# K tiles transposed as pairs of fp32 words, and a direct PV product, in a one-token decode kernel

## The chip, the core and the metric

The kernel runs on one core of one Trainium2 chip. The metric is the device time of one execution in microseconds; a time below is of one execution or the median of several. All inputs are bfloat16 and lie in HBM.

## What is computed

One token of a transformer block for a batch of B = 2: attention over a cache, then a gated feed-forward. The cache is what is large: K and V are each 2 x 32 heads x 8192 positions x 128 values, 134 MB each.

```
h  = x + A(layernorm(x))
q  = x @ wq                        -> [B, 32 heads, 1, 128]
s  = q . k_cache * 128**-0.5       -> [B, 32, 1, 8192]
o  = softmax(s) @ v_cache          -> [B, 32, 1, 128]
A  = o.reshape(B, 1, 4096) @ wo    (wo: 4096 x 512)
h2 = h + W_down(relu(W_gate(layernorm(h))) * W_up(layernorm(h)))     (F = 1376)
```

## The kernel before

**Tiling.** The work is cut into NP = 32 pairs; pair p is two neighbouring heads of one batch. The K tile of a pair has 128 partitions, 64 for each head; a partition holds J = 128 consecutive positions of its head, each with 128 values, so a tile is 128 x 32 KB = 4 MB, loaded by one DMA with 32 KB a partition. V has the same form. Four slots of SBUF hold tiles: K of even and odd pairs, V of even and odd pairs.

**Scores on two engines.** Of the J = 128 positions of a partition, 96 go to VectorE in NCH = 2 halves of JC = 48: a product with the broadcast q (L407), a tree of additions (L415), a reduction (L424). The other JP = 32 go to TensorE in NG = 4 groups of GT = 8 (L427 to L444): 8 transposes of 128x128 into a PSUM tile `Tp` (L434), one ScalarE copy to `kT` in SBUF (L440), and in `score_group` (L274) 8 products with `kT` as the stationary operand and two columns of q (`qT`) as the moving one. Two `Tp` tiles alternate, and three `kT`.

**Softmax and PV.** `exp` (L282) runs on ScalarE, part by part (the 32 positions of TensorE, then VectorE's halves), and writes `e_t`, two columns a position, one for each head, with zeros on the other head's partitions. `pv` (L341) multiplies it with V: for four positions at a time, the 8 columns of `e_t` are the stationary operand and 512 columns of V the moving one (L361); 32 such products of a pair go to four 32-row strips of a PSUM bank `Op`. Of each 8 x 512 result only the blocks are wanted in which position meets position. `collect` (L368), called one pair later, copies `Op` to SBUF in fp32 (`os_sb`, L372), and four fp32 products with a selecting matrix `sel` (L378) add the blocks into two columns of the bank `Ob`. For the last pair, `pv` takes the other form already: V's 128 x 128 blocks stationary, two columns of `e_t` moving (L354).

**Normalization and the rest.** After pairs 8, 16, 24 and 31, `z_sum` (L293) adds the exponentials' sums over the partitions with a product by ones, `normalize` (L300) reduces and inverts them on VectorE, and `o_scale` (L314) writes the scaled outputs `O_sb`. `o_proj` (L324) multiplies them with wo: for the first 24 heads after pair 24, for the rest at the end. Then come the residual, the feed-forward's products (L518, L560) and the output.

**The order of work.** The engines' instruction streams are written out by hand. Each engine runs its instructions in program order; `Prog` gives each engine a semaphore that counts its instructions, and `wait` makes an engine wait for another's count. All loads but x are issued by SyncE (SP) on one DMA queue, in this order:

- wq, K0, V0, K1, V1, a piece of W_down; then wo (L226) when the q product is done with wq's place;
- in the loop, for pair p: K of p+2 (L459 to L461), when the second VectorE product of p (L407) and the last transpose of p are done (`t_kfree`); then V of p+2 (`load_v`, L387), when `pv(p)` is done (`t_pv`);
- at pair 30: the weights W_up and W_gate in slot 0, V of pair 31 in four parts with semaphores of their own (`vparts`, L338), W_down.

**The last pairs.** In pair 31, `pv(30)` and `collect(30)` are issued after the TensorE scores and the first `exp` of pair 31 (L450 to L453), and `normalize(3)` stands within VectorE's tree of additions for the last half (L418). After the loop: `o_proj` for heads 24 to 31 without the last pair's batch, `z_sum` and `normalize` of the last pair, `pv(31)`, and what follows from it.

The two statements that differ most:

```
i = nc.tensor.transpose(Tp[n % 2][:, k * 128:(k + 1) * 128], k_t[:, j, :], ident[:])             # L434, x8 a group
i = nc.tensor.matmul(o[g:g + 2 * VJ, :], lhsT=e_t[p % 2][:, j:j + VJ, :]..., rhs=v_t[:, j:j + VJ, :]...)   # L361, x32 a pair
```

Of the kernel before, what the change touches and what calls it, by code (L numbers as in the profile page):

```python
# [6 lines left out]
F32 = mybir.dt.float32  # L7
BF16 = mybir.dt.bfloat16
ALU = mybir.AluOpType
ACT = mybir.ActivationFunctionType  # L10
# [28 lines left out]
def bass_sequential_preLN__gqa_block_cached__glu_gated_reglu__decode_kernel(  # L39
# [12 lines left out]
    B, _, D = A_x.shape  # L52
# [14 lines left out]
    VJ = 4  # L67
# [4 lines left out]
    with ExitStack() as es:  # L72
# [27 lines left out]
        qT = sb("qT", [128, NP * 2], BF16)  # L100
        ident = sb("ident", [128, 128], BF16)
# [47 lines left out]
        with nc.Block() as block:  # L149

            @block.sync
            def _(eng):
# [18 lines left out]
                pool.run(nc.gpsimd.memset(sel[:], 0.0))  # L171
                for c in range(4):
                    pool.last()
                    pool.run(nc.gpsimd.tensor_copy(
                        out=sel[32 * c:32 * c + 2 * VJ, :], in_=ident_f[0:2 * VJ, 0:2 * VJ]))
                pool.last()
# [24 lines left out]
                for k, row in enumerate((x_row, lnx_row)):  # L201
                    rv = row.rearrange("b (n c) -> b c n", c=DC)
                    for c in range(DC):
                        i = nc.tensor.transpose(
                            Tp[0][:, (k * DC + c) * B:(k * DC + c + 1) * B], rv[:, c, :], ident[0:B, 0:B])
                t = pe.run(i)
                dve.wait(t)
                t_xlT = dve.run(nc.vector.tensor_copy(out=xlT[:], in_=Tp[0][:, 0:2 * DC * B]))
# [6 lines left out]
                for h in range(H):  # L215
# [8 lines left out]
                    in_=Wp[:, 0:H * B].rearrange("p (g a b) -> p g b a", b=B, a=2)))  # L224
                sp.wait(t_q)
# [34 lines left out]
                t_os, t_ob = {}, {}  # L260
# [6 lines left out]
                def score_group(p, g):  # L267
                    n = p * NG + g
                    pe.wait(t_ev[n])
# [17 lines left out]
                def zbank(k):  # L287
                    return Sp[0] if k == 4 else Ob

                def zcol(k):  # L290
                    return 64 if k == 4 else 2 * NP

                def z_sum(k, p0, p1):  # L293
                    pe.wait(t_exp[p1 - 1][-1])
                    t = pe.run(nc.tensor.matmul(  # L295
                        zbank(k)[:, zcol(k):zcol(k) + (p1 - p0) * 2 * (NCH + 1)], lhsT=ones_f[:],
                        rhs=zs[:, 2 * p0:2 * p1, :], start=True, stop=True))
                    return t

                def normalize(k, p0, p1, t, split):  # L300
                    n = 2 * (p1 - p0)
                    dve.wait(t)
                    dve.run(nc.vector.tensor_reduce(
                        out=zr[:, 2 * p0:2 * p1],
                        in_=zbank(k)[:, zcol(k):zcol(k) + n * (NCH + 1)].rearrange("p (n k) -> p n k", k=NCH + 1),
                        axis=AX.X, op=ALU.add))
                    dve.last()
                    dve.run(nc.vector.reciprocal(out=zi[:, 2 * p0:2 * p1], in_=zr[:, 2 * p0:2 * p1]))
                    dve.last()
                    if split:  # L310
                        return None
                    return o_scale(k, p0, p1)

                def o_scale(k, p0, p1):  # L314
                    src = Op[1][:, 0:2] if k == 4 else Ob[:, 2 * p0:2 * p1]
                    return dve.run(nc.vector.tensor_tensor(
                        out=O_sb[:, 2 * p0:2 * p1], in0=src, in1=zi[:, 2 * p0:2 * p1],
                        op=ALU.mult))
# [22 lines left out]
                def pv(p):  # L341
                    v_t = tile((2 * p + 1) % 4)
                    o = Op[p % 2]
                    parts = vparts if p == NP - 1 else (
                        [(0, NCH * JC, J)] + [(1 + c, c * JC, (c + 1) * JC) for c in range(NCH)])
                    pe.wait(t_zero)
                    if p >= 2:
                        pe.wait(t_os[p - 2])
                    nmm = 0
                    for ci, (ei, j0, j1) in enumerate(parts):  # L350
                        pe.wait(t_exp[p][ei], (sem_vl[ci], 16) if p == NP - 1 else t_v[p])
                        if p == NP - 1:
                            for j in range(j0, j1):
                                i = nc.tensor.matmul(  # L354
                                    o[:, 0:2], lhsT=v_t[:, j, :], rhs=e_t[p % 2][:, j, :],
                                    start=(nmm == 0), stop=(nmm == J - 1))
                                nmm += 1
                            continue
                        for j in range(j0, j1, VJ):
                            g = 32 * (nmm % 4)  # L360
                            i = nc.tensor.matmul(  # L361
                                o[g:g + 2 * VJ, :], lhsT=e_t[p % 2][:, j:j + VJ, :].rearrange("p j a -> p (j a)"),
                                rhs=v_t[:, j:j + VJ, :].rearrange("p j d -> p (j d)"),
                                start=(nmm < 4), stop=(nmm >= J // VJ - 4))
                            nmm += 1
                    t_pv[p] = pe.run(i)

                def collect(p):  # L368
                    act.wait(t_pv[p])
                    if p >= 1:  # L370
                        act.wait(t_ob[p - 1])
                    t_os[p] = act.run(nc.scalar.activation(out=os_sb[:], in_=Op[p % 2][:], func=ACT.Copy))  # L372
                    k = next(kk for kk, (a, b_) in enumerate(batches) if a <= p < b_)
                    pe.wait(t_os[p])
                    if p == batches[k][0] and k >= 1:
                        pe.wait(t_O[k - 1])
                    for jj in range(VJ):
                        i = nc.tensor.matmul(  # L378
                            Ob[:, 2 * p:2 * p + 2], lhsT=os_sb[:, jj * Dh:(jj + 1) * Dh],
                            rhs=sel[:, 2 * jj:2 * jj + 2], start=(jj == 0), stop=(jj == VJ - 1))  # L380
                    t_ob[p] = pe.run(i)
# [17 lines left out]
                for p in range(NP):  # L399
# [3 lines left out]
                    for c in range(NCH):  # L403
                        dve.wait(t_k[p])
                        dve.last()
# [4 lines left out]
                        while w > 8:  # L410
# [7 lines left out]
                            if p == NP - 1 and c == 1 and w == Dh // 2:  # L418
                                t_O[3] = normalize(3, 24, 31, t_batch[3], False)
# [5 lines left out]
                        if c == 0:  # L425

                            pe.wait(t_k[p])  # L427
                            for g in range(NG):
                                n = p * NG + g
                                if n >= 2:  # L430
                                    pe.wait(t_ev[n - 2])
                                for k in range(GT):
                                    j = NCH * JC + g * GT + k
                                    i = nc.tensor.transpose(  # L434
                                        Tp[n % 2][:, k * 128:(k + 1) * 128], k_t[:, j, :], ident[:])
                                t_pt[n] = pe.run(i)
# [3 lines left out]
                                t_ev[n] = act.run(nc.scalar.activation(  # L440
                                    out=kT[n % 3][:], in_=Tp[n % 2][:], func=ACT.Copy))
# [8 lines left out]
                            if p == NP - 1:  # L450
                                pv(p - 1)
                            if p >= 1:
                                collect(p - 1)  # L453
# [29 lines left out]

                pe.wait(t_O[3])
# [121 lines left out]
```

## Time and profile before

| | us |
|---|---|
| three runs | 672.58, 672.62, 673.44 |
| median | 672.62 |
| the profiled execution: its time | 672.58 |
| its span in the profile | 670.7 |
| busy in the span: VectorE (DVE) | 494.4 (74%) |
| TensorE products (PE), its weight loads (PEld) | 352.0 (52%), 234.1 (35%) |
| ScalarE (ACT) | 220.1 (33%) |
| GpSimd (POOL) | 2.5 |
| data loaded | 281.06 MB |

The span runs from the program's first instruction to its last; 1.9 us of the time lie outside it. Busy time is the sum of an engine's instructions. TensorE's products and its weight loads are counted apart and overlap each other. The costliest groups, with the mean duration of one instruction:

| line | engine | what | count | busy us | mean ns |
|---|---|---|---|---|---|
| L407 | DVE | product with q, 128x6144 | 64 | 214.9 | 3358 |
| L440 | ACT | copy of transposed K, 128x1024 | 128 | 126.2 | 1021 |
| L434 | PE | transposes, 128x128 bf16 | 1024 | 122.0 | 305 |
| L361 | PE | PV, 8 columns stationary, 512 moving | 992 | 116.3 | 621 |
| L378 | PE | fp32 products of `collect` (two records for each call) | 248 | 57.5 | 354 |
| L274 | PE | scores, two moving columns | 1024 | 48.2 | 168 |
| L372 | ACT | copy of `Op`, 128x512 fp32 | 31 | 18.5 | 597 |
| L354 | PE | PV of the last pair, two moving columns | 128 | 3.7 | 166 |

Means of TensorE are from an instruction's start to its modelled end. Products follow each other faster than that: 8 transposes take 1.01 us in the timeline, 80 products of L354 take 2.27 us.

### The profile page before, as it was taken

The page shows a single profiled execution, that of the slowest core. Times are in us where ns is not written, and L with a number is a line of the kernel's source. Part 1 is how long each engine was busy: PE and PEld are TensorE (multiplying, and loading weights), DVE is VectorE, ACT ScalarE, POOL GpSimd, SP SyncE. Part 2 cuts the span into 40 slices and gives each one's busy share as a digit, 9 for nine tenths or more (in the row PEclk, how much of TensorE's full clock was granted, in tenths as well). Part 3 has the DMA queues.
Part 4 walks back from the last instruction along what each step waited for, and adds up shares of the span by engine and source line. Part 5 has one row for each costly group of instructions (what it writes and reads, how often), then busy time and mean ns, then how long its engine had stood idle before and what let it go on. Part 6 is the DMA issues. An engine that isn't in the chain of part 4 may idle for free.

```text
span 670.7 us, 8986 instructions
## 1 busy us (share of the span) xinstructions
PE 352.0 (52%) x3868; PEld 234.1 (35%) x3868; DVE 494.4 (74%) x430; ACT 220.1 (33%) x554; POOL 2.5 (0%) x16
## 2 busy tenths in 40 slices
PE   2553355455545455554554655454556565455655
PEld 2431333233433223343322433232234443223435
DVE  1774477788768678877777887677786977678792
ACT  0631322233432234344222333322333342233340
POOL 1000000000000000000000000000000000000000
PEclk9999999665565555655556656655566555565555
DMA  9999999999999999999999999999999999999994
GB/s 375 434 436 357 434 435 430 427 431 429 434 433 427 428 433 433 425 436 425 434 433 427 431 436 424 431 432 431 437 426 425 434 432 433 426 430 431 428 409 146
DMA packets 15915, 281.63 MB, mean 420 GB/s; under 512 B 1442, under 2 KB 6916, under 8 KB 7044
## 3 DMA queue, kind: packets, MB, share of 16 engines
q1 hardware_dynamic: 15872, 281.06, 98.4%
q8 instruction: 30, 0.49, 0.3%
q14 instruction: 9, 0.07, 0.0%
q10 hardware_dynamic: 4, 0.00, 0.0%
HBM read 281.05 MB, written 0.00 MB: 419 GB/s over the span
## 4 chain that ended last, share of the span: by engine, by line
DMA 72%; DVE 22%; PE 3%; ACT 2%; issue 1%; SPq 0%; DVEq 0%
DMA slot<-in_A_k_cache_dram 68%; DVE prod L407 14%; DVE tb L415 4%; DMA slot<-in_A_v_cache_dram 3%; DVE prod L415 2%; ACT kT L440 1%; DVE scores L424 1%; PE T L434 1%; PE Ob L378 1%; ACT e L282 0%; PE S L274 0%; ACT os_sb L372 0%; PE Ob L295 0%; PE S L518 0%; PE O L560 0%
## 5 line engine op out<-in xcount | busy, mean ns | idle before, releaser
L407 DVE TENSOR_TENSOR prod<-slot,q_b 128x6144 bf16<-128x6144 bf16 x64 | 214.9, 3358 | 128.2 <-DMA slot<-in_A_k_cache_dram 126.9
L361 PE MATMUL O<-slot,e 128*8 128x512 bf16 x992 | 116.3, 621 | 143.4 <-ACT e L282 127.8
L440 ACT ACTIVATE kT<-T 128x1024 bf16<-128x1024 bf16 x128 | 126.2, 1021 | 160.2 <-PE T L434 159.4
L434 PE MATMUL T<-ident,slot 128*128 128x128 bf16 x1024 | 122.0, 305 | 65.3 <-DMA slot<-in_A_k_cache_dram 65.3
L415 DVE TENSOR_TENSOR tb<-prod 128x3072 bf16<-128x3072 bf16 (+1 forms) x128 | 148.2, 1158 | 4.4
L434 PEld LDWEIGHTS T<-ident,slot 128*128 128x128 bf16 x1024 | 99.3, 140 | 92.3 <-DMA slot<-in_A_k_cache_dram 90.6
L282 ACT ACTIVATE e<-scores 64x48 bf16<-64x48 f32 x128 | 32.8, 256 | 239.2 <-DVE scores L424 237.6
L361 PEld LDWEIGHTS O<-slot,e 128*8 128x8 bf16 x992 | 24.0, 106 | 209.6 <-ACT e L282 155.6
L415 DVE TENSOR_TENSOR prod<-tb 128x1536 bf16<-128x1536 bf16 (+1 forms) x128 | 84.2, 658 | 4.4
L378 PE MATMUL Ob<-sel,os_sb 128*128 128x2 f32 x248 | 57.5, 354 | 47.7 <-ACT os_sb L372 47.7
L378 PEld LDWEIGHTS Ob<-sel,os_sb 128*128 128x128 f32 x248 | 54.9, 327 | 51.2 <-ACT os_sb L372 51.2
L274 PE MATMUL S<-qT,kT 128*128 128x2 bf16 x1024 | 48.2, 168 | 39.2 <-ACT kT L440 38.1
L274 PEld LDWEIGHTS S<-qT,kT 128*128 128x128 bf16 x1024 | 40.7, 106 | 57.5 <-ACT kT L440 57.5
L424 DVE TENSOR_REDUCE scores<-prod 128x48 f32<-128x384 bf16 x64 | 35.4, 553 | 2.2
L282 ACT ACTIVATION_READ_ACCUMULATOR e<-scores 64x1 f32 x128 | 23.6, 185 | 0.0
L372 ACT ACTIVATE os_sb<-O 128x512 f32<-128x512 f32 x31 | 18.5, 597 | 3.4 <-PE O L361 2.7
L282 ACT ACTIVATE e<-S 64x32 bf16<-64x32 f32 x64 | 12.9, 202 | 15.0 <-PE S L274 14.2
L282 ACT ACTIVATION_READ_ACCUMULATOR e<-S 64x1 f32 x64 | 12.8, 201 | 0.7
L251 ACT ACTIVATE q_b<-O 128x512 bf16<-128x512 f32 x8 | 4.3, 595 | 15.8 <-PE O L246 15.8
L222 DVE CAST qT<-W 128x64 bf16<-128x64 f32 x1 | 0.2, 224 | 12.2 <-PE W L217 12.2
L217 PE MATMUL W<-xlT,X 128*128 128x2 bf16 x128 | 3.6, 166 | 8.8 <-DMA X<-in_A_wq_dram 8.8
L217 PEld LDWEIGHTS W<-xlT,X 128*128 128x128 bf16 x128 | 3.5, 104 | 8.8 <-DMA X<-in_A_wq_dram 8.8
(67 smaller groups left out, 58.8 us busy)
## 6 DMA issues: line engine op xcount, KB each, us to landing
slot<-in_A_k_cache_dram SPq DMA_DIRECT2D x32, 4096.0 KB, 27.7
slot<-in_A_v_cache_dram SPq DMA_DIRECT2D x31, 4096.0 KB, 31.3
X<-in_A_wq_dram SPq DMA_DIRECT2D x1, 4096.0 KB, 12.5
X<-in_A_wo_dram SPq DMA_DIRECT2D x1, 4096.0 KB, 48.7
slot<-in_A_v_cache_dram SPq DMA_DIRECT2D x1, 1536.0 KB, 19.8
slot<-in_B_W_up_dram SPq DMA_DIRECT2D x1, 1376.0 KB, 10.0
slot<-in_B_W_gate_dram SPq DMA_DIRECT2D x1, 1376.0 KB, 14.6
slot<-in_A_v_cache_dram SPq DMA_DIRECT2D x1, 1280.0 KB, 22.2
```

The source lines that it names most:

```text
L217: i = nc.tensor.matmul(Wp[:, h * B:(h + 1) * B], lhsT=wq[:, c, h * Dh:(h + 1) * Dh], rhs=lT[:, c * B:(c + 1) * B], start=(c == 0), stop=(c ...
L251: t_cp[m] = act.run(nc.scalar.activation(out=q_b[:, m * 512:(m + 1) * 512], in_=Op[m % 2][:], func=ACT.Copy))
L274: i = nc.tensor.matmul(Sp[p % 2][:, 2 * jj:2 * jj + 2], lhsT=kT[n % 3][:, k * 128:(k + 1) * 128], rhs=qT[:, 2 * p:2 * p + 2], start=True, ...
L282: t = act.run(nc.scalar.activation(out=e_t[p % 2][q, j0:j0 + nj, a], in_=src(q, a), func=ACT.Exp, scale=inv_sqrt_dh, accum_out=zs[q, 2 * p ...
L361: i = nc.tensor.matmul(o[g:g + 2 * VJ, :], lhsT=e_t[p % 2][:, j:j + VJ, :].rearrange("p j a -> p (j a)"), rhs=v_t[:, j:j + VJ, :].rearrang ...
L372: t_os[p] = act.run(nc.scalar.activation(out=os_sb[:], in_=Op[p % 2][:], func=ACT.Copy))
L378: i = nc.tensor.matmul(Ob[:, 2 * p:2 * p + 2], lhsT=os_sb[:, jj * Dh:(jj + 1) * Dh], rhs=sel[:, 2 * jj:2 * jj + 2], start=(jj == 0), stop= ...
L407: t_dm = dve.run(nc.vector.tensor_tensor(out=prod[:], in0=k_t[:, c * JC:(c + 1) * JC, :], in1=qv, op=ALU.mult))
L415: dve.run(nc.vector.tensor_tensor(out=o, in0=cur[:, :, 0:half], in1=cur[:, :, half:w], op=ALU.add))
L424: t_s = dve.run(nc.vector.tensor_reduce(out=sc[:], in_=cur, axis=AX.X, op=ALU.add))
L434: i = nc.tensor.transpose(Tp[n % 2][:, k * 128:(k + 1) * 128], k_t[:, j, :], ident[:])
L440: t_ev[n] = act.run(nc.scalar.activation(out=kT[n % 3][:], in_=Tp[n % 2][:], func=ACT.Copy))
```

## The change

**Transposes.** Two positions of a K tile, 2 x 128 bf16 values, are taken as 128 fp32 words and transposed by one fp32 transpose with the fp32 identity, 4 a group in place of 8. In the result, row n holds the values 2n and 2n+1 of the even position's head vector in rows 0 to 63 and of the odd position's in rows 64 to 127. `Tp` becomes three fp32 tiles (`Ob`'s bank is free now), read by the same copy as bf16.

**Scores.** For each two positions there are two products, r = 0 for even and r = 1 for odd places in the head vector, accumulated into four columns (two positions x two heads). The moving operand is `q2`, 4 columns for each pair and r: q's even or odd values in rows 0 to 63 for the first position and in rows 64 to 127 for the second, and zeros elsewhere. `q2` is made at the start by four products with every second column of the identity, a memset and four copies on VectorE. The number of products is as before, 8 a group.

**PV.** All pairs take the form that only the last one had: V's 128 x 128 block of each position stationary, two columns of `e_t` moving, 128 products of a pair, accumulated into the pair's two columns of `Op[k % 2]` for its batch k. `collect`, `os_sb`, `sel`, `Ob` and the memsets of `Op` are gone. `z_sum` and `normalize` of a batch now follow `pv` of its last pair directly; in the last pair, `pv(30)` and `normalize(3)` come after the loop.

The diff, cut to its core:

```diff
+        q2 = sb("q2", [128, NP, 2, 4], BF16)
-        os_sb = sb("os_sb", [128, 512], F32)
-        sel = sb("sel", [128, VJ * 2], F32)
-        Tp = [ps(f"T{i}", [128, GT * 128], BF16) for i in range(2)]
+        Tp = [ps(f"T{i}", [128, GT * 64], F32) for i in range(3)]
-        Ob = ps("Ob", [128, 512], F32)
...
+                pe.wait(t_qT)
+                for r in range(2):
+                    for h in range(2):
+                        i = nc.tensor.matmul(
+                            Sp[r][64 * h:64 * h + 64, 0:2 * NP], lhsT=ident[:].rearrange("p (n r) -> p r n", r=2)[:, r, :],
+                            rhs=qT[:], start=True, stop=True)
+                t = pe.run(i)
+                dve.run(nc.vector.memset(q2[:], 0.0))
+                dve.wait(t)
+                dve.last()
+                for r in range(2):
+                    for h in range(2):
+                        t_q2 = dve.run(nc.vector.tensor_copy(
+                            out=q2[64 * h:64 * h + 64, :, r, 2 * h:2 * h + 2],
+                            in_=Sp[r][64 * h:64 * h + 64, 0:2 * NP].rearrange("p (n a) -> p n a", a=2)))
...
-                dve.wait(t_cp[NP // 4 - 2], t_cp[NP // 4 - 1])
-                for o in Op:
-                    t_zero = dve.run(nc.vector.memset(o[:], 0.0))
...
-                    for k in range(GT):
-                        jj = g * GT + k
-                        i = nc.tensor.matmul(
-                            Sp[p % 2][:, 2 * jj:2 * jj + 2], lhsT=kT[n % 3][:, k * 128:(k + 1) * 128],
-                            rhs=qT[:, 2 * p:2 * p + 2], start=True, stop=True)
+                    kv_ = kT[n % 3][:].rearrange("p (k n r) -> p k r n", n=128, r=2)
+                    for k in range(GT // 2):
+                        jj = g * GT + 2 * k
+                        for r in range(2):
+                            i = nc.tensor.matmul(
+                                Sp[p % 2][:, 2 * jj:2 * jj + 4], lhsT=kv_[:, k, r, :],
+                                rhs=q2[:, p, r, :], start=(r == 0), stop=(r == 1))
...
-                        for j in range(j0, j1, VJ):
-                            g = 32 * (nmm % 4)
+                        for j in range(j0, j1):
                             i = nc.tensor.matmul(
-                                o[g:g + 2 * VJ, :], lhsT=e_t[p % 2][:, j:j + VJ, :].rearrange("p j a -> p (j a)"),
-                                rhs=v_t[:, j:j + VJ, :].rearrange("p j d -> p (j d)"),
-                                start=(nmm < 4), stop=(nmm >= J // VJ - 4))
+                                Op[k % 2][:, col:col + 2], lhsT=v_t[:, j, :], rhs=e_t[p % 2][:, j, :],
+                                start=(nmm == 0), stop=(nmm == J - 1))
                             nmm += 1
                     t_pv[p] = pe.run(i)
-
-                def collect(p):
-                    act.wait(t_pv[p])
...
-                    t_os[p] = act.run(nc.scalar.activation(out=os_sb[:], in_=Op[p % 2][:], func=ACT.Copy))
...
-                    if p + 1 in ends:
+                    if p + 1 in ends and p < NP - 1:
                         t_batch[k] = z_sum(k, *batches[k])
...
+                        if p == 0 and c == 0:
+                            dve.wait(t_cp[NP // 4 - 1])
...
-                            if p == NP - 1 and c == 1 and w == Dh // 2:
-                                t_O[3] = normalize(3, 24, 31, t_batch[3], False)
...
-                                if n >= 2:
-                                    pe.wait(t_ev[n - 2])
-                                for k in range(GT):
-                                    j = NCH * JC + g * GT + k
+                                if n >= 3:
+                                    pe.wait(t_ev[n - 3])
+                                for k in range(GT // 2):
+                                    j = NCH * JC + g * GT + 2 * k
                                     i = nc.tensor.transpose(
-                                        Tp[n % 2][:, k * 128:(k + 1) * 128], k_t[:, j, :], ident[:])
+                                        Tp[n % 3][:, k * 128:(k + 1) * 128],
+                                        k_t[:, j:j + 2, :].rearrange("p j d -> p (j d)").bitcast(F32), ident_f[:])
...
-                            if p == NP - 1:
-                                pv(p - 1)
-                            if p >= 1:
-                                collect(p - 1)
...
+                pv(NP - 2)
+                t_O[3] = normalize(3, 24, 31, t_batch[3], False)
                 pe.wait(t_O[3])
```

More of the change, by code (lines that the diff above doesn't have):

```diff
@@ L66, in bass_sequential_preLN__gqa_block_cached__glu_gated_reglu__decode_kernel @@
     FR = F - 10 * 128
-    VJ = 4
     eps = 1e-5
@@ L170, in _ @@
                 pool.run(nc.gpsimd.memset(onesn[:], 1.0 / D))
[L171 to L176, printed above, removed]
                 for e in e_t:
@@ L204, in _ @@
                         i = nc.tensor.transpose(
-                            Tp[0][:, (k * DC + c) * B:(k * DC + c + 1) * B], rv[:, c, :], ident[0:B, 0:B])
+                            Tp[0][:].bitcast(BF16)[:, (k * DC + c) * B:(k * DC + c + 1) * B], rv[:, c, :], ident[0:B, 0:B])
                 t = pe.run(i)
                 dve.wait(t)
-                t_xlT = dve.run(nc.vector.tensor_copy(out=xlT[:], in_=Tp[0][:, 0:2 * DC * B]))
+                t_xlT = dve.run(nc.vector.tensor_copy(out=xlT[:], in_=Tp[0][:].bitcast(BF16)[:, 0:2 * DC * B]))
                 xT = xlT[:, 0:DC * B]
@@ L252, in _ @@
                         out=q_b[:, m * 512:(m + 1) * 512], in_=Op[m % 2][:], func=ACT.Copy))
-                dve.wait(t_cp[NP // 4 - 2], t_cp[NP // 4 - 1])
-                for o in Op:
-                    t_zero = dve.run(nc.vector.memset(o[:], 0.0))
                 t_pt, t_ev, t_sc, t_pv = {}, {}, {}, {}
-                t_os, t_ob = {}, {}
                 t_exp = {}
@@ L268, in score_group @@
                     n = p * NG + g
-                    pe.wait(t_ev[n])
+                    pe.wait(t_ev[n], t_q2)
                     if g == 0 and p >= 2:
                         pe.wait(t_exp[p - 2][0])
-                    for k in range(GT):
-                        jj = g * GT + k
-                        i = nc.tensor.matmul(
-                            Sp[p % 2][:, 2 * jj:2 * jj + 2], lhsT=kT[n % 3][:, k * 128:(k + 1) * 128],
-                            rhs=qT[:, 2 * p:2 * p + 2], start=True, stop=True)
+                    kv_ = kT[n % 3][:].rearrange("p (k n r) -> p k r n", n=128, r=2)
[5 more added lines that the diff above has]
+                                rhs=q2[:, p, r, :], start=(r == 0), stop=(r == 1))
                     t_sc[n] = pe.run(i)
@@ L287, in zbank @@
                 def zbank(k):
-                    return Sp[0] if k == 4 else Ob
-                def zcol(k):
-                    return 64 if k == 4 else 2 * NP
+                    return Sp[0] if k == 4 else Op[k % 2]
                 def z_sum(k, p0, p1):
@@ L295, in z_sum @@
                     t = pe.run(nc.tensor.matmul(
-                        zbank(k)[:, zcol(k):zcol(k) + (p1 - p0) * 2 * (NCH + 1)], lhsT=ones_f[:],
+                        zbank(k)[:, 64:64 + (p1 - p0) * 2 * (NCH + 1)], lhsT=ones_f[:],
                         rhs=zs[:, 2 * p0:2 * p1, :], start=True, stop=True))
@@ L304, in normalize @@
                         out=zr[:, 2 * p0:2 * p1],
-                        in_=zbank(k)[:, zcol(k):zcol(k) + n * (NCH + 1)].rearrange("p (n k) -> p n k", k=NCH + 1),
+                        in_=zbank(k)[:, 64:64 + n * (NCH + 1)].rearrange("p (n k) -> p n k", k=NCH + 1),
                         axis=AX.X, op=ALU.add))
@@ L314, in o_scale @@
                 def o_scale(k, p0, p1):
-                    src = Op[1][:, 0:2] if k == 4 else Ob[:, 2 * p0:2 * p1]
                     return dve.run(nc.vector.tensor_tensor(
-                        out=O_sb[:, 2 * p0:2 * p1], in0=src, in1=zi[:, 2 * p0:2 * p1],
+                        out=O_sb[:, 2 * p0:2 * p1], in0=Op[k % 2][:, 0:2 * (p1 - p0)], in1=zi[:, 2 * p0:2 * p1],
                         op=ALU.mult))
@@ L342, in pv @@
                     v_t = tile((2 * p + 1) % 4)
-                    o = Op[p % 2]
+                    k = next(kk for kk, (a, b_) in enumerate(batches) if a <= p < b_)
+                    col = 2 * (p - batches[k][0])
                     parts = vparts if p == NP - 1 else (
                         [(0, NCH * JC, J)] + [(1 + c, c * JC, (c + 1) * JC) for c in range(NCH)])
-                    pe.wait(t_zero)
-                    if p >= 2:
-                        pe.wait(t_os[p - 2])
+                    if p == batches[k][0] and k >= 2:
+                        pe.wait(t_O[k - 2])
                     nmm = 0
@@ L351, in pv @@
                         pe.wait(t_exp[p][ei], (sem_vl[ci], 16) if p == NP - 1 else t_v[p])
-                        if p == NP - 1:
[L353 to L358, printed above, removed]
-                        for j in range(j0, j1, VJ):
-                            g = 32 * (nmm % 4)
+                        for j in range(j0, j1):
                             i = nc.tensor.matmul(
-                                o[g:g + 2 * VJ, :], lhsT=e_t[p % 2][:, j:j + VJ, :].rearrange("p j a -> p (j a)"),
-                                rhs=v_t[:, j:j + VJ, :].rearrange("p j d -> p (j d)"),
-                                start=(nmm < 4), stop=(nmm >= J // VJ - 4))
+                                Op[k % 2][:, col:col + 2], lhsT=v_t[:, j, :], rhs=e_t[p % 2][:, j, :],
+                                start=(nmm == 0), stop=(nmm == J - 1))
                             nmm += 1
                     t_pv[p] = pe.run(i)
-                def collect(p):
-                    act.wait(t_pv[p])
-                    if p >= 1:
-                        act.wait(t_ob[p - 1])
-                    t_os[p] = act.run(nc.scalar.activation(out=os_sb[:], in_=Op[p % 2][:], func=ACT.Copy))
[L373 to L381, printed above, removed]
-                    if p + 1 in ends:
+                    if p + 1 in ends and p < NP - 1:
                         t_batch[k] = z_sum(k, *batches[k])
@@ L440, in _ @@
                                 t_ev[n] = act.run(nc.scalar.activation(
-                                    out=kT[n % 3][:], in_=Tp[n % 2][:], func=ACT.Copy))
+                                    out=kT[n % 3][:], in_=Tp[n % 3][:].bitcast(BF16), func=ACT.Copy))
                                 if g >= 1:
@@ L449, in _ @@
                                 NCH * JC, JP)
-                            if p == NP - 1:
-                                pv(p - 1)
-                            if p >= 1:
-                                collect(p - 1)
                         act.wait(t_s)
```

## The prediction

> **What bounds the kernel now.** I read first the slices and the queues of the page, to see which resource has no idle time.
>
> ```profile
> DMA  9999999999999999999999999999999999999994
> ...
> q1 hardware_dynamic: 15872, 281.06, 98.4%
> q8 instruction: 30, 0.49, 0.3%
> ```
>
> The transfers fill every slice but the last: 281.06 MB, 98.4% of all 16 DMA engines' time. The second queue row matters below: 30 packets of 16 KB of instructions, 0.3% of 16 x 670.7 us = 32 us, so 1.07 us each.
>
> Second, stretches of three pairs each, inside the loop (columns: length; busy time and count of PE, PEld, DVE, ACT, POOL; TensorE clock; DMA share; GB/s).
>
> ```profile
> 218.32:276.61 58.29, 31.24 (x313) 20.03 (x312) 44.25 (x36) 20.05 (x51) 0.00 (x0) 0.53 1.00 431
> 276.61:334.90 58.29, 31.73 (x312) 20.41 (x312) 44.78 (x36) 19.56 (x51) 0.00 (x0) 0.51 1.00 430
> ```
>
> DMA share 1.00; DVE is busy 44.8 of 58.3 us, PE 31.7, ACT 20. One pair (8.39 MB) takes 19.43 us, and DVE idles about 4.5 us in it, PE about 9. No compute engine sets the pace.
>
> Third, the chain that ended last, where DVE starts on K tiles 10, 12, 14, 18, 20, 22, 24, 26, 28, 30 right after they land (columns: start, length, what):
>
> ```profile
> 232.31 3.37 DVE prod L407
> ...
> 271.16 3.37 DVE prod L407
> ...
> 310.02 3.37 DVE prod L407
> ...
> 388.25 3.37 DVE prod L407
> ...
> 428.14 3.37 DVE prod L407
> ...
> 467.00 3.37 DVE prod L407
> ...
> 506.33 0.05 issue
> ...
> 545.24 3.37 DVE prod L407
> ...
> 585.12 3.37 DVE prod L407
> ...
> 623.98 3.37 DVE prod L407
> ```
>
> The clean step for two pairs is 38.86 us (232.31 to 271.16, 271.16 to 310.02). But 310.02 to 388.25 is 0.51 us more than two such steps, 388.25 to 428.14 is 1.03 more, 467.00 to 506.33 is 0.47 more, 545.24 to 585.12 is 1.02 more: 391.67 us for ten steps where 388.6 would do. Some 3.1 us are lost, in jumps. The trace's DMA packets tell why. For a whole load, the moments at which the 16 DMA engines finished their shares (us after the first of them), by when the last finished:
>
> ```
>  42.97  0.00 0.09 0.10 0.14 0.16 0.18 0.28 0.36 0.40 0.40 0.42 0.45 0.66 0.82 1.64 1.78
> 211.37  0.00 0.11 0.33 0.37 0.38 0.41 0.85 1.18 1.70 1.71 1.73 1.85 1.85 2.02 2.16 2.37
> 222.11  0.00 0.12 0.32 0.37 0.38 0.41 0.86 1.18 1.70 1.72 1.72 1.85 2.01 2.17 2.38 3.40
> 623.50  0.00 0.07 0.12 0.16 0.28 0.59 2.80 4.02 4.58 4.68 4.82 4.85 5.16 5.39 6.24 6.41
> ```
>
> Between rows two and three lies one instruction packet, at 215.7 us, and one engine went from 1.85 to 3.40. Each such packet costs its engine 1.54 us (the 1.08 us packet, and 0.48 us by which a 32 KB data packet beside it is longer than its usual 1.22). An engine never makes this up, as all 16 stream without a gap, and a load has landed only when the slowest is done. From 43.0 to 623.5 us the slowest engine fell back 4.63 us, during 24 packets of PE instructions: **0.193 us a packet**. That is 1.54/8: followed from load to load, the jumps go round some eight engines, while six stay within 0.6 us. So the kernel's time is its data at 9.714 us per 4 MB load, plus what instruction packets take from the unluckiest engine, plus a start and a tail.
>
> **The change, part by part.** I add to the profiled execution: span 670.7, timed at 672.58 us (the lowest; the median of the three is 672.62).
>
> *TensorE's instructions.* The page counts 3868 matmuls and as many weight loads; 7736 / 30 = 258 a packet, so a packet holds 256. Removed: 992 wide PV products (L361), 248 records of the 124 fp32 products of `collect` (L378), 512 of the 1024 transposes. Score products stay 1024 (L274: before 8 a group, after 4 x 2). Added: 31 x 128 = 3968 PV products and 4 for q2. New count 3868 - 992 - 248 - 512 + 3968 + 4 = 6088, with weight loads 12176, so 4440 instructions more: **17.3 packets**. The trace shows no fp32 transpose. If it has two records a call, as L378 has, the count is 21.3 packets; if one, as L434, 17.3. I take one: L434 is the same operation. Price: 17.3 x 0.193 = **+3.3 us**. Spread over all 16 engines it would be 17.3 x 1.54 / 16 = +1.7; with 21.3 packets and a third hit on the slowest engine, 3 x 1.54 = +4.6.
>
> The Trainium skill speaks against this term. "Runtime: NRT & Kernel Launch", section "Instruction fetch mechanics", has the refill in blocks of 256 instructions, as the packets here, and calls the cost of crossing a block "mostly hidden". That is said of the engine that runs them; by it this term is nothing and the sum 672.7. The row at 222.11 shows who pays: the data stream.
>
> *TensorE's time*, beside the transfers. PV of a pair before: 20 products in 2.31 us and 12 in 1.45 (timeline), then 1.87 us for L378. After: 128 as L354 does them for the last pair, 80 in 2.27 us, so 3.6 us. Transposes: 8 in 1.01 us now; 16 calls take 2.0 us at that rate, or 16 x 0.47 = 7.5 at L378's rate for an fp32 call (8 records in 1.87 us). Scores: 32 products as now, 1.5 us a pair, though their weights are now every second column; at L378's rate, as an upper bound, 7.5. Even the worst sum, 18.6, stays under 19.43. Cost 0. Cover: the 19.43 us period. Of ScalarE, 31 copies of 597 ns (L372) go; ScalarE waits for DVE anyway. Worth 0.
>
> *The queue's waits.* SP issues K of pair p+2 after the second L407 and the last transpose, V after `pv(p)`:
>
> ```profile
> 282.29 0.33 SPq L139 DMA_DIRECT2D slot<-in_A_k_cache_dram  x1
> 288.89 0.33 SPq L139 DMA_DIRECT2D slot<-in_A_v_cache_dram  x1
> ```
>
> K of the next pair but one lands at 310.0, a load takes 9.7, so the issue at 282.3 is 18 us early; V's is over 20 early. `pv` still ends after the second `exp` of the scores (its last 48 products, 1.4 us, against 12 in 1.45), and transposes at worst 5 us later still end before the second L407, 11 us after landing. An engine 10 us ahead of the slowest still finds work. Cost 0; if 8 us of it were lost, the fast engines would idle first, not the slowest.
>
> *`normalize` in the loop* (three times) now stands in DVE's queue behind the second half of a pair, not within the next. The next L407 waits behind it for `pv` and a sum, about 2 us, in 4 idle. Cost 0. *The start*: DVE gets a memset and four small copies (0.2 to 0.5 us each) and loses two memsets of 485 ns; by 63 us of queued loads ahead of K of pair 2 it is free.
>
> *The tail.* The last lines before:
>
> ```profile
> 655.05 0.55 DVE L424 TENSOR_REDUCE scores<-prod 128x48 f32<-128x384 bf16 x1
> ...
> 656.82 2.27 PE L354 MATMUL O<-e,slot 128*128 128x2 bf16 x80
> ...
> 659.34 1.44 PE L354 MATMUL O<-e,slot 128*128 128x2 bf16 x48 [0.25 <-DMA slot<-in_A_v_cache_dram]
> ```
>
> PE waits for V at 659.34 and ends at 660.78; the way from DVE's end at 655.60 has 0.25 us to spare. After, `normalize(3)` leaves the middle of DVE's chain (652.36 to 653.07: 0.71 us), so DVE ends 0.71 earlier, but then comes behind it (0.71), then 32 products of L328 (1.23), z_sum with 0.44 until PV starts, 128 products (3.65): 655.60 - 0.71 + 0.05 + 0.71 + 1.23 + 0.44 + 3.65 = 660.98, 0.2 behind the old end. V itself comes up to 0.2 later against K, by the packets between. I take **+0.1**; bounds 0 and +0.7 (no overlap between L328 and z_sum).
>
> Sum: 672.58 + 3.3 + 0.1 = **676.0 us**.
>
> **Rivals.** *Not slower*: the extra packets fall on engines that are not the last. The six that are within 0.6 us at 623.5 could take 17.3 / 6 = 2.9 hits, 4.4 us, and still end before 6.41. Then only the tail counts: 672.7. It decides at one hit: a single 1.54 us on the slowest engine is already over 0.2% (1.35 us, about what a measurement of this kernel can tell from no change). Against it: 24 packets in a row left those six alone. 0.11. *TensorE becomes the bound*: if each PV product cost its unhidden weight load (106 ns, L354), 128 take 13.6 us, with 7.5 of transposes and 1.5 of scores 22.6 a pair, 3.2 over the period, 770 us. Against it: L354's 28 ns each. 0.03. *Faster*: the 0.7 us that `normalize` gives back to DVE is all that could be won at the end, 0.1%, and it needs free packets; something unseen must add to it. 0.03. *Twice-recorded fp32 transposes*: 21.3 x 0.193 = 4.1, so 676.8; inside the forecast's range.
>
> **How the numbers follow.** Forecast (with the last rival) 0.83: 676.0. The range goes from 672.58 + 1.7 - 0.1 = 674.2 to 672.58 + 4.6 + 0.7 = 677.9. It leaves out the other cases, 0.17. Slower 0.86 (with the TensorE case), within 0.2% 0.11, faster 0.03.
>
> **What would show it.** In the profile after: q8 with 47 or 48 packets (51 or 52 if two records a transpose) in place of 30; clean steps of 38.86 us between K tiles two pairs apart, with more jumps; the slowest DMA engine near 9.7 us behind at the 30th K tile; the last V some 3 us later, the tail behind it as now; DMA share 1.00 throughout. Wrong if q8 grows and K tiles do not come later, or if a stretch shows DMA below 1.00 with DVE or PE full.

## The result, and the profile after

The changed kernel takes 676.26 us (median; 676.0 to 676.45), the kernel before 672.79 us in the same comparison: a ratio of 1.005, with a 95% interval of 1.0032 to 1.0067. The forecast was 676.0. The profiled execution after took 676.18 us, with a span of 674.2 us, 3.5 more than before.

The line numbers move: the product with q is L384 now (it was L407), the transposes are L409 (L434), the scores L277 (L274), PV is L352 (L361 and L354). The queue rows and the slices of the page after:

```profile
DMA  9999999999999999999999999999999999999993
...
q1 hardware_dynamic: 15872, 281.06, 98.0%
q8 instruction: 47, 0.77, 0.5%
```

The data are the same to the byte, the transfers fill every slice but the last, and there are 17 more packets of TensorE instructions (47 for 30). The stretches inside the loop (length; busy time and count of PE, PEld, DVE, ACT, POOL; TensorE clock; DMA share; GB/s):

```profile
218.32:276.61 58.29, 25.60 (x518) 22.66 (x519) 44.01 (x36) 17.23 (x48) 0.00 (x0) 0.50 1.00 430
276.61:334.90 58.29, 26.40 (x530) 22.99 (x529) 45.00 (x37) 18.12 (x49) 0.00 (x0) 0.50 1.00 429
```

TensorE and ScalarE are busy for less of a stretch, 26 us for 31.5 and 17.7 for 19.8, but TensorE with 1.7 times the instructions. Neither was waited for, so nothing is gained. The chain after, with the K tiles 10, 12, 14 to 30 at VectorE (start, length, what):

```profile
232.45 3.37 DVE prod L384
...
272.58 3.37 DVE prod L384
...
311.70 3.37 DVE prod L384
...
350.56 3.37 DVE prod L384
...
390.89 3.37 DVE prod L384
...
508.94 3.37 DVE prod L384
...
547.87 3.37 DVE prod L384
...
627.02 3.37 DVE prod L384
```

The clean step of 38.86 us is still there (311.70 to 350.56). Ten steps take 394.57 us, 5.97 more than 388.6; before it was 3.07 more. The steps that lose are now up to 1.47 us too long (350.56 to 390.89, and 232.45 to 272.58 by 1.27). K tile 30 starts 3.04 us later than before. The finishing times of the 16 DMA engines on two loads, the second that of K tile 30, from the trace's DMA packets (time at which the last engine is done; then, for each engine, us after the first):

```
222.27  0.00 0.17 0.22 0.29 0.41 0.47 0.66 1.23 1.63 1.67 3.24 3.25 3.28 3.29 3.47 3.59
626.53  0.00 0.19 0.31 0.36 0.48 0.96 2.98 4.21 7.74 7.81 7.88 7.88 8.22 9.38 9.51 9.69
```

Eight engines have moved together: on K tile 30's load they were 4.6 to 6.4 us behind before and are 7.7 to 9.7 behind now. The slowest is 9.69 us behind where it was 6.41 behind (row 623.50 in the prediction). The engine that finishes first does so at 616.85 us, before at 617.09: the transfers as such have not become slower. The last stretch of the timeline (start, length, engine, line, what):

```profile
657.49 0.55 DVE L399 TENSOR_REDUCE scores<-prod 128x48 f32<-128x384 bf16 x1
...
660.20 2.27 PE L352 MATMUL O<-e,slot 128*128 128x2 bf16 x80
...
662.81 1.44 PE L352 MATMUL O<-e,slot 128*128 128x2 bf16 x48 [0.34 <-DMA slot<-in_A_v_cache_dram]
```

TensorE waits for the last V again, 0.34 us (0.25 before), so VectorE's and TensorE's own way to this point has not become the one that ends last. From 662.81 to the end of the span it is 11.4 us, as it was from 659.34.

### The profile page after: what moved, and what is told of

It reads as the page before. It is cut to its first block, busy times and chain, and to the rows that moved or that the text cites. A ratio compares the mean times of both kernels' runs of the same rounds, so it can differ in the third digit from the quotient of the medians.

```text
span 674.2 us, 13420 instructions
## 1 busy us (share of the span) xinstructions
PE 302.7 (45%) x6088; PEld 264.7 (39%) x6088; DVE 494.6 (73%) x433; ACT 202.6 (30%) x523; POOL 1.7 (0%) x11
## 4 chain that ended last, share of the span: by engine, by line
DMA 73%; DVE 25%; PE 1%; issue 1%; SPq 0%; DVEq 0%
DMA slot<-in_A_k_cache_dram 69%; DVE prod L384 15%; DVE tb L392 5%; DMA slot<-in_A_v_cache_dram 3%; DVE prod L392 3%; DVE scores L399 1%; PE S L492 0%; PE O L534 0%; PE O L352 0%; SPq L371 0%; SPq L136 0%; SPq L447 0%; PE W L492 0%; PE O L492 0%; PE W L327 0%
## 5 line engine op out<-in xcount | busy, mean ns | idle before, releaser
L384 DVE TENSOR_TENSOR prod<-slot,q_b 128x6144 bf16<-128x6144 bf16 x64 | 214.9, 3358 | 130.7 <-DMA slot<-in_A_k_cache_dram 127.9
L352 PE MATMUL O<-e,slot 128*128 128x2 bf16 x4096 | 118.6, 166 | 233.1 <-ACT e L285 120.5
L352 PEld LDWEIGHTS O<-e,slot 128*128 128x128 bf16 x4096 | 114.5, 104 | 237.4 <-ACT e L285 129.1
L409 PE MATMUL T<-ident_f,slot 128*128 128x128 f32 x512 | 131.7, 425 | 72.7 <-DMA slot<-in_A_k_cache_dram 72.6
L409 PEld LDWEIGHTS T<-ident_f,slot 128*128 128x128 f32 x512 | 95.2, 218 | 75.7 <-DMA slot<-in_A_k_cache_dram 75.7
L392 DVE TENSOR_TENSOR prod<-tb 128x1536 bf16<-128x1536 bf16 (+1 forms) x128 | 84.2, 658 | 4.4
L277 PEld LDWEIGHTS S<-q,kT 128*128 128x128 bf16 x1024 | 42.7, 108 | 67.7 <-ACT kT L416 65.8
L277 PE MATMUL S<-q,kT 128*128 128x4 bf16 x1024 | 48.8, 170 | 39.0 <-ACT kT L416 39.0
L327 PE MATMUL W<-O_sb,X 128*128 128x2 bf16 (+1 forms) x136 | 5.0, 173 | 6.8 <-DVE O_sb L315 6.8
L327 PEld LDWEIGHTS W<-O_sb,X 128*128 128x128 bf16 x136 | 4.8, 118 | 7.1 <-DVE O_sb L315 7.1
```

What stands on the lines that cost most here:

```text
L277: i = nc.tensor.matmul(Sp[p % 2][:, 2 * jj:2 * jj + 4], lhsT=kv_[:, k, r, :], rhs=q2[:, p, r, :], start=(r == 0), stop=(r == 1))
L327: i = nc.tensor.matmul(Wp[:, c * B + b0:c * B + b1], lhsT=wo_m[:, h, c, :], rhs=Ov[:, h // 2, h % 2, b0:b1], start=first[0], stop=last, sk ...
L352: i = nc.tensor.matmul(Op[k % 2][:, col:col + 2], lhsT=v_t[:, j, :], rhs=e_t[p % 2][:, j, :], start=(nmm == 0), stop=(nmm == J - 1))
L384: t_dm = dve.run(nc.vector.tensor_tensor(out=prod[:], in0=k_t[:, c * JC:(c + 1) * JC, :], in1=qv, op=ALU.mult))
L392: dve.run(nc.vector.tensor_tensor(out=o, in0=cur[:, :, 0:half], in1=cur[:, :, half:w], op=ALU.add))
L409: i = nc.tensor.transpose(Tp[n % 3][:, k * 128:(k + 1) * 128], k_t[:, j:j + 2, :].rearrange("p j d -> p (j d)").bitcast(F32), ident_f[:])
```

## The experiments

The theory: the loss is made by the packets that bring TensorE's instructions, each of which holds up one of some eight DMA engines, and the slowest engine sets when a load has landed. The rivals: PV with V as the stationary operand, or the fp32 transposes, slow the transfers or delay the release of a slot; or TensorE's work as such does it. Each time stands beside the kernel before on the same chip.

**e1_more_pe: only as many instructions.**

```diff
                         pv(p)
+                        for _ in range(74):
+                            i = nc.tensor.matmul(
+                                Tp[0][:].bitcast(F32)[:, 0:2], lhsT=ident[:], rhs=qT[:, 0:2], start=True, stop=True)
```

> The kernel before, with 74 small products (ident stationary, two columns of q moving, into a Tp bank that is free) added behind pv(p) for pairs 0 to 29: 2220 products, so 4440 more TensorE instructions, as many as the change adds, and nothing else of the change. Theory (instruction packets): 47 or 48 packets on the second queue in place of 30, K tile 30 some 3.3 us later, time 3.3 us over the kernel before (bounds 2.6 to 4.6), so about 676. Rival (V as the stationary operand of 3968 products, or the fp32 transposes, slow the transfers): neither is in this kernel, so the time of the kernel before, within 0.5 us.

Measured: 676.46 us against 672.97, +3.49; ratio 1.0052, interval 1.0039 to 1.0065. The queue's row and K tile 30 in the chain:

```profile
q8 instruction: 47, 0.77, 0.5%
```

```profile
627.21 3.37 DVE prod L407
```

The same packets as after the change, K tile 30 at 627.21 for 627.02, the same time. Nothing of the change is in this kernel but its number of instructions, and that is enough for the whole loss. The first engine is done with K tile 30's load at 617.05 us here, as in the kernel before, and the slowest 9.63 us later.

**e2_transposes: only the fp32 transposes and the scores.** The diff is that of the change for `q2`, `score_group`, the transposes and the type of `Tp`; `Tp` keeps two tiles, and PV, `collect` and `normalize` stay as before:

```diff
-        Tp = [ps(f"T{i}", [128, GT * 128], BF16) for i in range(2)]
+        Tp = [ps(f"T{i}", [128, GT * 64], F32) for i in range(2)]
...
-                                for k in range(GT):
-                                    j = NCH * JC + g * GT + k
+                                for k in range(GT // 2):
+                                    j = NCH * JC + g * GT + 2 * k
                                     i = nc.tensor.transpose(
-                                        Tp[n % 2][:, k * 128:(k + 1) * 128], k_t[:, j, :], ident[:])
+                                        Tp[n % 2][:, k * 128:(k + 1) * 128],
+                                        k_t[:, j:j + 2, :].rearrange("p j d -> p (j d)").bitcast(F32), ident_f[:])
```

> Only the fp32 transposes and the block-diagonal scores of the change; PV, collect and normalize as before. TensorE then has 508 products fewer, 1016 instructions, 4 packets: 26 on the second queue. Theory: 4 x 0.193 = 0.8 us less than before, about 671.9; K tiles not later anywhere. Rival (the fp32 transposes cost the transfers something, or delay the release of the K slots): 1 to 3 us more than before.

Measured: 671.67 us against 672.97, -1.30; ratio 0.9981, interval 0.9972 to 0.999. 26 packets:

```profile
q8 instruction: 26, 0.43, 0.3%
```

```profile
622.71 3.37 DVE prod L425
```

This half of the change makes the kernel faster, and it is the fastest of all that ran: it beats both the kernel before and the changed one. The gain is somewhat over the 0.8 us that 0.193 a packet gives. The engines show how: at a load done at 622.24 the slowest is 5.24 us behind the first, for 6.41 before, so 1.17 less. An engine is hit by whole packets of 1.54 us. Followed from load to load, the slowest has three hits before, from 1.86 us behind, and two here, from 2.00 us behind.

**e3_pv: only the PV half.** The changed kernel with the transposes and scores of before:

```diff
-        Tp = [ps(f"T{i}", [128, GT * 64], F32) for i in range(3)]
+        Tp = [ps(f"T{i}", [128, GT * 128], BF16) for i in range(3)]
...
-                                for k in range(GT // 2):
-                                    j = NCH * JC + g * GT + 2 * k
+                                for k in range(GT):
+                                    j = NCH * JC + g * GT + k
                                     i = nc.tensor.transpose(
-                                        Tp[n % 3][:, k * 128:(k + 1) * 128],
-                                        k_t[:, j:j + 2, :].rearrange("p j d -> p (j d)").bitcast(F32), ident_f[:])
+                                        Tp[n % 3][:, k * 128:(k + 1) * 128], k_t[:, j, :], ident[:])
```

> Only the PV half of the change (V stationary, no collect, normalize behind pv, pv(30) and normalize(3) after the loop); bf16 transposes and scores as before. 2728 products more, 5456 instructions, 21.3 packets: 51 or 52 on the second queue. Theory: 21.3 x 0.193 = 4.1 us, with the tail's 0.1 about 676.8, so some 0.8 us over the whole change. Rival (the transposes cause part of the loss): less than the whole change's 3.5 us.

Measured: 677.39 us against 672.97, +4.42; ratio 1.0068, interval 1.0056 to 1.0081; 51 packets. The PV half alone loses more than the whole change; the transposes give about 1 us of it back. The rival that blames the transposes falls.

**e5_twice_pe: twice the dose.** As e1 with `range(148)`.

> As the first experiment, with 148 small products behind each pv(p) in place of 74: 8880 more TensorE instructions than before, 34.7 packets, 64 or 65 on the second queue. Theory: twice the loss, 34.7 x 0.193 = 6.7 us over the kernel before (the first dose measured 3.5, so 7.0 by it). TensorE is still idle for 5 us of each pair. Rival (a loss that comes once, when some engine first runs out of queued work or a wait moves): the same 3.5 us.

Measured: 679.2 us against 672.78, +6.42; ratio 1.0094, interval 1.0081 to 1.0107.

```profile
q8 instruction: 65, 1.06, 0.6%
```

The loss doubles, nearly (3.49, 6.42; the theory had 6.7). It is no wait that comes once.

**e7_wide: TensorE's time without the instructions.**

```diff
                         pv(p)
+                        for _ in range(8):
+                            i = nc.tensor.matmul(
+                                Tp[0][:].bitcast(F32), lhsT=ident[:], rhs=q_b[:, 0:512], start=True, stop=True)
```

> The kernel before, with 8 products of 512 moving columns behind pv(p) for pairs 0 to 29: 240 products, 480 instructions, 1.9 packets, but about 0.43 us of TensorE each at half clock, so 3.4 us a pair against the 2.1 us of the 74 small products. Theory: 1.9 x 0.193 = 0.4 us over before. Rival (it is TensorE's time, power or its reads of SBUF that slow the transfers, not its instructions): 3.5 us or more.

Measured: 672.94 us against 672.78, +0.16; ratio 1.0, interval 0.9992 to 1.0009; 32 packets. The 240 products are busy for 99.0 us in the profile, the 2220 small ones of e1 for 63.9: more of TensorE's time than in e1, and it costs the transfers nothing that can be measured. The weight loads are few here, 240 for 2220; that these slow the transfers by their reads is not tested by this run, but the first engine's time in e1 speaks against it.

**The five doses and the change together.** K tile 30 is when VectorE starts on it; the last column is against the kernel before in the same comparison.

| kernel | TensorE instructions | packets | K tile 30 at, us | median us | us over before |
|---|---|---|---|---|---|
| e2_transposes | 6720 | 26 | 622.71 | 671.67 | -1.30 |
| before | 7736 | 30 | 623.98 | 672.62 | 0 |
| e7_wide | 8216 | 32 | 624.13 | 672.94 | +0.16 |
| e1_more_pe | 12176 | 47 | 627.21 | 676.46 | +3.49 |
| the change | 12176 | 47 | 627.02 | 676.26 | +3.47 |
| e3_pv | 13192 | 51 | 627.40 | 677.39 | +4.42 |
| e5_twice_pe | 16616 | 65 | 629.97 | 679.2 | +6.42 |

From 26 to 65 packets the time grows by 7.72 us, 0.198 us a packet, whatever the instructions are for.

**e4_pool: instructions on an idle engine.**

```diff
                         pv(p)
+                        pool.wait(t_pv[p])
+                        pool.last()
+                        for c in range(64):
+                            t = pool.run(nc.gpsimd.memset(junk[:, c:c + 1], 0.0))
```

> The kernel before, with 64 memsets of one bf16 column on GpSimd behind pv(p) for pairs 0 to 29: 1920 instructions on an engine that is otherwise idle and that nobody waits for. GpSimd then must fetch instructions too. In the trace of before, 8 KB packets of ScalarE and VectorE instructions (9 in all) put one engine each back by 0.7 to 1.0 us, always the same two. Theory: 15 packets of 8 KB, all on one DMA engine, which falls back 10 to 15 us where the slowest now is at 6.4; time 4 to 9 us over before if that engine carries no PE packets. Rival (what counts is the bytes, shared by all 16 engines: 123 KB at 430 GB/s): 0.3 us over before, not measurable.

Measured: 676.87 us against 672.97, +3.90; ratio 1.006, interval 1.0047 to 1.0072. The rows of its queues, and the group of the memsets (count, busy us, mean ns, idle before):

```profile
q8 instruction: 30, 0.49, 0.3%
q14 instruction: 24, 0.20, 0.1%
```

```profile
L468 POOL MEMSET junk<- 128x1 bf16 x1920 | 65.3, 101 | 559.4 <-PE O L362 559.4
```

TensorE's packets are as before; 15 packets of 8 KB are new. 65 us of memsets, spread over the span on an engine that nobody waits for, cost 3.9 us, just under the theory's lower end of 4. By bytes shared it would be 0.3. In the trace's DMA packets one engine alone runs away:

```
211.84  0.00 0.01 0.04 0.12 0.15 0.75 1.05 1.42 1.55 1.58 1.63 1.74 1.77 1.89 1.89 2.77
488.57  0.00 0.06 0.12 0.16 0.28 2.20 3.07 3.10 3.18 3.25 3.34 4.57 5.00 5.08 5.09 7.62
```

Its steps (4.23 to 4.88, 4.89 to 5.54, 5.55 to 6.21 in loads between) are 0.65 us a packet. On K tile 30's load it is 10.2 us behind the first engine, the next 6.5: that is 3.8 more than the 6.4 of the slowest engine before, and so nearly the whole loss.

**e6_eight: take load off the engines that are hit.** On e2, wo in parts; the wait for wo is raised to the five DMAs' count:

```diff
-                nc.sync.dma_start(
-                    X[:].rearrange("p (h n) -> p h n", n=D),
-                    A_wo.rearrange("(h d) n -> d h n", d=128)).then_inc(sem_wo, 16)
+                for d0, d1 in ((0, 96), (96, 104), (104, 112), (112, 120), (120, 128)):
+                    nc.sync.dma_start(
+                        X[d0:d1, :].rearrange("p (h n) -> p h n", n=D),
+                        A_wo.rearrange("(h d) n -> d h n", d=128)[d0:d1]).then_inc(sem_wo, 16)
```

> The kernel with the transposes alone (671.67 us), with the load of wo cut: 96 partitions in one DMA, then four DMAs of 8 partitions. By the Trainium skill (DMA: Bandwidth & Descriptors, section on why a DMA increments its semaphore by 16) a DMA of 8 partitions runs on the 8 lowest-numbered engines. From the trace alone: wo costs an engine 256 packets of 1 KB at 48 ns, 12.3 us; if four DMAs of 8 partitions go to one half of the engines, that half does 10 parts of 8, 3.1 us more, and the other half 6, 3.1 us less. Theory (the end is set by the slowest engine, which the instruction packets make): if the engines with TensorE packets are the upper half, 2.5 to 3.1 us less than 671.7; if they are the lower half, 3 us more; if they are mixed, up to 3 us more. Rival (the sum of bytes counts, spread over all): 671.7 within 0.5.

Measured: 696.87 us against 672.78, +24; the runs lie from 690.72 to 698.61. No theory expected that. In the profiled execution (690.81 us) the DMA packets show where it goes: the 1 KB packets of wo, which take 51 ns (median) in the kernel before and in e2, take 80 to 87 ns here from the first part on, and 130 to 147 ns after 70 us, and the last of them ends at 84.2 us in place of 65.1. SP's own timeline (start, length, issue), here and then of the kernel before:

```profile
16.55 50.11 SPq L243 DMA_DIRECT2D X<-in_A_wo_dram  x5
66.78 3.58 SPq L140 DMA_DIRECT2D slot<-in_A_k_cache_dram  x1
```

```profile
16.87 0.39 SPq L226 DMA_DIRECT2D X<-in_A_wo_dram  x1
35.96 23.68 SPq L139 DMA_DIRECT2D slot<-in_A_k_cache_dram  x1
```

SP was held in issuing the parts of wo until 66.7 us, and the issue of K of pair 2 ended at 70.4 in place of 59.6. The hold explains little of the loss, for from 51 to 65 us the DMA engines were busy throughout (DMA share 1.11) with the slow packets; from 65 to 70 us the share was 0.70. Two slices of the page fall to 191 and 179 GB/s; K tile 10 starts at 250.45 us, 19.4 later than in e2. After that the loop runs as before: 391.57 us from K tile 10 to 30, for 391.68 in e2. So the experiment says nothing on evening out the engines. Why wo's packets became slower, and what spreads the times over 8 us, stays open. After wo, eight engines are 3 us and more behind the other eight, and engines of both halves go on being hit (one of the first eight goes from 0.09 to 1.65 us behind, one of the last eight from 5.39 to 6.95), so a cut into halves could not have worked in this form.

## Why the prediction was right

*The bound.* Right: DMA share 1.00 in the stretches shown, the clean step of 38.86 us unchanged, 2.90 us of the 3.47 in steps that are too long.

*Instructions to packets.* Right: 4440 more instructions in the count, 12176 on the page after (6088 products and as many weight loads), 17 more packets for 17.3. An fp32 transpose has one record: 512 in the group of L409. The value taken was the right one of the two; no trace ahead of the result could tell.

*The price of a packet.* Predicted 0.193 us on the slowest engine, so +3.3. The medians say 3.47 for 17 packets, 0.204; the row of doses 0.198. Between K tiles 10 and 30 the loss was 2.90, before K tile 10 0.14, after K tile 30 0.43: the slowest engine moves in jumps of whole packets, so a short stretch tells less than the whole. The slowest engine is 9.69 us behind on K tile 30's load, as forecast (near 9.7). The bound of +1.7 for packets spread over all 16 engines is excluded, and so is the rival in which they fall on engines that are not the last. Three slips of the prediction carry nothing: 1.08 and 0.48 make 1.56 and not 1.54 (its rows have 1.55), the times of the tail add up to 660.97 and not 660.98, and the range's lower end takes 0.1 off for a tail whose lower bound is given as 0.

*The rule of the Trainium skill.* "Runtime: NRT & Kernel Launch", section "Instruction fetch mechanics", calls the cost of a block boundary "mostly hidden". For TensorE itself nothing here speaks against it: in the timeline of a pair in the loop PE's idle time ends with DMA or ScalarE. For a kernel that the transfers bound it does not hold: e1 pays 3.49 us for such blocks and nothing else. The measurement decides.

*TensorE's time.* Right in the end, with one size in between its bounds. The lines of a pair in the loop after (start, length, engine, line, what):

```profile
311.72 1.97 PE L409 MATMUL T<-ident_f,slot 128*128 128x128 f32 x8 [1.87 <-DMA slot<-in_A_k_cache_dram]
...
314.19 1.09 PE L409 MATMUL T<-ident_f,slot 128*128 128x128 f32 x4
...
315.34 1.09 PE L409 MATMUL T<-ident_f,slot 128*128 128x128 f32 x4
...
321.52 2.27 PE L352 MATMUL O<-e,slot 128*128 128x2 bf16 x80 [3.60 <-DMA slot<-in_A_v_cache_dram]
...
327.95 1.44 PE L352 MATMUL O<-e,slot 128*128 128x2 bf16 x48 [4.16 <-ACT e L285]
```

The 16 fp32 transposes take 1.97, 1.09 and 1.09, so 4.2 us a pair, not the 2.0 of the lower bound. Of the bf16 ones, eight took 1.01 and a pair's 32 took 3.9, so a pair's transposes cost TensorE about what they did. PV takes 2.27 and 1.44 us, as forecast from the last pair before.

*The tail.* V came 3.47 us later and K tile 30 3.04, so V and not VectorE's chain ended last again. From V on, the way to the end is as long as before. Against K, V came 0.43 later, where the prediction allowed 0.2; why stays open. The sum is close in part by luck: up to K tile 30 the loss was 3.04 and not 3.3, behind it 0.43 and not 0.1, and the two offset. That `normalize(3)` moved was not tried alone.

*The queue's waits.* Right where it mattered, but "still finds work" failed once. Near the end V of pair 30 is not issued at pair 28, as the order given above has it, but at pair 29, behind K of pair 31, so fewer loads are queued there. SP issues K of pair 31 at 618.74 us, and the first engines were done with K tile 30's load from 616.85 on: a slice late in the span has 398 GB/s where before it had 431. The first engine ends the next load 13.0 us after this one, the slowest 9.8 us, for 9.71 of a load. So, as the prediction argued, the fast engines idle and not the slowest.

## What to carry to other kernels

In a kernel whose transfers never pause, count instructions: the blocks of code come through the same DMA engines as the data, and the engine that fetches most sets when each load has landed. Read it in the instruction rows of the queues, in steps between equal loads that are not equal, and in the spread of the engines' finishing times. A form with fewer, wider instructions can be worth more than one that is faster on its engine: here fp32 transposes of pairs were a gain, the PV product of 128 small pieces a loss.

## What the runs showed of the hardware that was not expected

- An instruction of GpSimd cost this kernel more than one of TensorE: 1920 memsets cost 3.9 us, 4440 TensorE instructions 3.5. GpSimd's packets are 8 KB and all go to one DMA engine (0.65 us each); TensorE's are 16 KB and go round some eight (1.54 us each). The Trainium skill ("Runtime: NRT & Kernel Launch", section "Instruction fetch mechanics") gives blocks of 16 KiB; in the traces the packets of the other instruction queue, GpSimd's in e4 and by their number ScalarE's and VectorE's, have 8 KB.
- SP can be held for long in issuing a DMA while earlier loads are under way: 23.7 us for K of pair 2 in the kernel before, 50.1 us for wo in five parts. In the first case no slice shows idle transfers; in the second wo itself ended 19 us later, with slower 1 KB packets (80 to 147 ns for 51).
- A 128x128 fp32 transpose takes 0.27 us in a row of four, about twice a bf16 one in a row of eight (0.13), and moves twice the data.
